# An attention block feeding a dense block on one core: when each load is issued, who fills the holes, and where block 1's decays stand

## The chip, the cores and the metric

The kernel runs on one core of a Trainium2 chip. The metric is the device time of one execution in microseconds; three runs of the kernel before gave 671.39 us in the median (670.71 to 673.25).

TensorE (PE) multiplies matrices into PSUM, VectorE (DVE) and ScalarE (ACT) work on tiles in SBUF and PSUM, GpSimd (POOL) is a fourth compute engine, and SyncE (SP) issues DMAs. ACT and POOL can issue DMAs too; each engine's instructions, DMA triggers included, are taken in the order in which they stand in its program.

## The reference

Two blocks in a row. The first is a linear attention with a decay per channel (RWKV-6), the second a dense layer with the activation `h - tanh(h)`:

```python
# r, k, v, w: (4, 8, 768, 48); u: (8, 48)
for t in range(S):
    cur = np.einsum('bhd,bhe->bhde', u[None] * kt, vt)
    y[:, :, t] = np.einsum('bhd,bhde->bhe', rt, state + cur)
    state = wt[:, :, :, None] * state + np.einsum('bhd,bhe->bhde', kt, vt)
...
x = attn_out.transpose(0, 2, 1, 3).reshape(4 * 768, 384)
h = x @ w_in            # 384 x 2048
out = (h - np.tanh(h)) @ w_out   # 2048 x 384
```

The attention's inputs and the output are float32; the dense weights come as float64.

## The kernel before

**Tiling.** The 3072 tokens are cut into 8 blocks of 384 (4 batches, 2 halves). The heads are worked on as 4 pairs, each pair on 128 partitions of which 96 carry data. Within a block, chunks of 64 tokens are solved by a tree: `level 1` and then levels m = 2, 4, 8, 16, 32 fill a matrix of scores from products of `kq` and `rp` (matmuls L242, and L319 for m = 32). After each level `decay` (L274) multiplies `kq` and `rp` in place by the running products of the decays, which `totals` (L260) makes from `wt`. Then `turn` transposes `kq` (L342, copied out at L344), `update` carries the state from chunk to chunk (L360, then DVE's chain of small operations L371), and `result` (L391, L409) makes the block's output, copied by ACT at L422 into `xT`, the input of the dense part. `late` holds the part of the output that does not fit the layout; six small DMAs of 24 KB (`fill_holes`, L429) put it into the holes of `xT`.

**Dense part.** For each block there are 16 steps f. A step has the product `hp` (L469) with one slice of `w_in`, six ACT operations (h, s, qa, qb, th, big, L476 to L481), five DVE operations that give `gT` (L486 to L494), and three steps later the products `acc` (L507) with one slice of `w_out`. `hp` has one PSUM buffer, so the next product waits until h has been read. At the end L512 copies `acc` out and a DMA stores it.

**Weights.** The float64 weights are read as pairs of 32-bit words, in 16 slices of 768 KB (`raw`, five buffers). `convert` turns a slice into float32 with two ACT operations (L170, L172) and two DVE operations (L174, L175).

**Order.** PE, SP, DVE and ACT run in the order in which the program emits; no scheduler moves anything on them. First `boot` does the whole attention of block 0 (in two halves of two pairs, `HALVES`), with the loads for block 1 and the first weights spread through it: `begin_behind(ins, dma)` makes a DMA wait for an instruction. In boot, six slices of weights are converted. Then, during the 16 dense steps of block i, the attention of block i + 1 runs a phase at a time: `plan(i)` says at which step each phase stands (`steps`), what DVE prepares before or behind a phase (`before`, `behind`), which steps convert a slice (`converted`), and which load is issued at which step (`loads`). In step f the order of emission is: `hp` and ACT's six operations of f, DVE's five operations of step f - 1 (with DVE's part of a conversion between them), what stands in `before`, the phase, what stands in `behind`, the load, ACT's part of a conversion, and `acc` of step f - 3.

All loads go through SP's queue, which is in order: a load that waits holds back everything behind it. Block 0's holes are filled by SP and ACT in turn, those of the other blocks by SP. Only block 0's step list (`i == 0`) has weights to load and convert.

Of the kernel before, what the change touches and what calls it, by code (L numbers as in the profile page):

```python
# [37 lines left out]
F32 = mybir.dt.float32  # L38
I32 = mybir.dt.int32
# [9 lines left out]
P = 128  # L49
# [35 lines left out]
def kernel(  # L85
# [23 lines left out]
    shift = const.tile([P, 3], F32, name="shift", tag="shift")  # L109
    for i, value in enumerate((QUAD[0][0], QUAD[1][0], -SMALL)):  # L110
        nc.vector.memset(shift[:, i:i + 1], value)

    warm = const.tile([P, 1], F32, name="warm", tag="warm")
    nc.scalar.activation(out=warm, in_=shift[:, 0:1], func=AF.Copy)
    u_sb = const.tile([P, NPAIR], F32, name="u_sb", tag="u_sb")
    nc.sync.dma_start(out=u_sb, in_=uT)


    masks = {}
# [63 lines left out]
    class Block:  # L183
# [16 lines left out]
        def load_v(self):  # L200
            self.v = inp.tile([P, NCP, DM], F32, name="v_sb", tag="v_sb")
            src = v[self.b, self.q * NB:(self.q + 1) * NB]
            nc.sync.dma_start(out=self.v, in_=src.rearrange("(c t) e -> t c e", t=P))

        def begin(self):
            self.xT = xpool.tile([P, KC, NB], F32, name="xT", tag="xT")
# [169 lines left out]
        def result(self, ps, pairs, holes_full=False):  # L376


            St, rp = states[self.q], self.tiles["rp"]
            yp = [scratch(ps) for e in range(2)]  # L380
            slots = [pairs[n:n + 2] for n in range(0, len(pairs), 2)]
            for n, slot in enumerate(slots):
                for c in range(NCP):
                    for par in range(2):
                        for p in slot:
                            for h in range(2):
                                rows = slice(64 * h, 64 * h + D)
# [12 lines left out]
            for n, slot in enumerate(slots):  # L400
                for p in slot:
                    for c in range(NCP):
                        for h in range(2):
                            for par in range(2):
                                toks = slice(64 * par, 64 * par + 64)
                                e0 = 64 * (h ^ (p % 2))
                                f0 = p * D2 + h * D
                                n0 = (n * NCP + c) * L
                                nc.tensor.matmul(yp[p % 2][e0:e0 + D, par, n0:n0 + L],  # L409
                                                 lhsT=self.v[toks, c, f0:f0 + D],  # L410
                                                 rhs=A[toks, h, p, c, :],
                                                 start=False,
                                                 stop=(n == len(slots) - 1 and c == NCP - 1),
                                                 skip_group_check=True)
            for n, slot in reversed(list(enumerate(slots))):
                for p in reversed(slot):
                    src = yp[p % 2][:, :, n * NCP * L:(n + 1) * NCP * L].rearrange(
                        "e a (c t) -> e c a t", t=L)
                    dst = self.xT[:, p, :] if p < KC else self.late
                    dst = dst.rearrange("e (c a t) -> e c a t", a=2, t=L)  # L420
                    for rows in (slice(0, D), slice(64, 64 + D)) if holes_full else (slice(0, P),):
                        nc.scalar.copy(out=dst[rows], in_=src[rows])  # L422

        def fill_holes(self, engines):

# [40 lines left out]
    def first(xT, f, ps):  # L466
        hp = ps.tile([P, NB], F32, name="hp", tag="hp")
        for kc in reversed(range(KC)):
            nc.tensor.matmul(hp, lhsT=w_in_sb[:, f, kc, :], rhs=xT[:, kc, :],  # L469
                             start=(kc == KC - 1), stop=(kc == 0))  # L470

        def new(name):
            return dense.tile([P, NB], F32, name=name, tag=name)

        h, th, s, qa, qb, big = (new(n) for n in ("h", "th", "s", "qa", "qb", "big"))
        nc.scalar.activation(out=h, in_=hp, func=AF.Copy, scale=1.0 / UPSCALE)  # L476
        nc.scalar.activation(out=s, in_=h, func=AF.Square)  # L477
        nc.scalar.activation(out=qa, in_=s, func=AF.Square, bias=shift[:, 0:1])  # L478
        nc.scalar.activation(out=qb, in_=s, func=AF.Square, bias=shift[:, 1:2])  # L479
        nc.scalar.activation(out=th, in_=h, func=AF.Tanh)  # L480
        nc.scalar.activation(out=big, in_=s, func=AF.Relu, bias=shift[:, 2:3])  # L481
        hs = dense.tile([P, NB], F32, name="hs", tag="hs", bufs=2)
        g = gpool.tile([P, NB], F32, name="gT", tag="gT")

        def product(out, in0, scalar, in1, op0):
            return lambda: nc.vector.scalar_tensor_tensor(out=out, in0=in0, scalar=scalar, in1=in1,  # L486
                                                          op0=op0, op1=ALU.mult)

        return g, [
            product(hs, h, SERIES, s, ALU.mult),  # L490
            lambda: nc.vector.tensor_tensor(out=th, in0=h, in1=th, op=ALU.subtract),  # L491
            product(hs, qa, QUAD[0][1], hs, ALU.add),
            product(g, qb, QUAD[1][1], hs, ALU.add),
            lambda: nc.vector.copy_predicated(out=g, mask=big.bitcast(I32), data=th)]  # L494

    class Second:

# [18 lines left out]
    def plan(i):  # L516

        names = ("level 1", 2, 4, 8, 16, 32, "turn", "update", "result")
        if i == 0:

            steps = (1, 2, 3, 4, 6, 8, 10, 11, 13)
            before = {0: ("totals 1", "totals 2", "kq")}
            behind, converted = {1: ("rp",)}, (0, 3, 3, 4, 4, 6, 10, 10, 12, 13)
            loads = {2: "weights", 5: "weights", 6: "weights", 7: "weights", 8: "weights",
                     9: "rmix", 10: "kmix", 11: "wt", 13: "kq", 14: "rp", 15: "v"}
        else:
            steps = (4, 5, 6, 7, 8, 9, 10, 11, 13)
            before = {0: ("kmix",), 1: ("rmix",), 2: ("totals 1",), 3: ("totals 2", "kq"), 4: ("rp",)}
            behind, converted = {}, ()
            loads = {5: "rmix", 7: "kmix", 9: "wt", 11: "kq", 14: "rp", 15: "v"}  # L530
        return dict(zip(steps, names)), before, behind, converted, loads

    blocks = [Block(b, q) for b in range(B) for q in range(NQ)]
# [16 lines left out]
    def boot(ps, blk, later):  # L550
# [21 lines left out]
        for m in (2, 4, 8, 16):  # L572
            blk.totals(m, h1, UP)
        masked()
        background = [lambda: later.load("rmix", rT, 0, NPAIR), lambda: later.load("kmix", kT, 0, NPAIR),
                      lambda: later.load("wt", wT, 0, NPAIR)] + [lambda: more_weights(nc.sync)] * 2
        ready, last = [], []
        for m in (2, 4, 8, 16, 32):
            for p0 in HALVES:
                if (m, p0) != (2, h1):  # L580
                    ins = blk.level(ps, m, p0, UP, last)
                if p0 == h2 or m == 32:
                    blk.totals(m, p0, UP)
            begin_behind(ins, background.pop(0)())
            if m <= 8:
                ready.append(convert(*raws.pop(0)))
            if m == 8:
# [2 lines left out]
        def converted():  # L590
            for op in ready.pop(0):
                op()

        for p0 in HALVES:
            blk.turn(ps, p0)
        for copies in last:
            copies()
        later.mix(0, NPAIR, ("kmix",))
        begin_behind(blk.update(ps, h1), later.load("kq", kT, 0, NPAIR))
        blk.update(ps, h2)  # L600
        blk.result(ps, [h1, h1 + 1])
        blk.fill_holes([nc.sync, nc.scalar])
        converted()
        ready.append(convert(*raws.pop(0)))
        more_weights(nc.sync)
        converted()
        blk.result(ps, [h2, h2 + 1], True)
        later.load("rp", rT, 0, NPAIR)
        more_weights(nc.sync)
        later.load_v()  # L610
        for _ in range(2):
            ready.append(convert(*raws.pop(0)))
        while ready:
            converted()
            more_weights(nc.sync)

    with tc.tile_pool(name="ps_boot", bufs=4, space=PSUM) as ps_boot:
        xT = blocks[0].begin()
# [4 lines left out]
    for i, blk in enumerate(blocks):  # L623
# [5 lines left out]
        phases, before, behind, converted, loads = plan(i)  # L629
        second = Second(blk.b * S + blk.q * NB, ps_d)  # L630
        for f in range(NF):
            g, next_rest = first(here, f, ps_d)
            waiting.append((second, f, g))

            for n, op in enumerate(rest):
# [6 lines left out]
            if later:  # L642
# [3 lines left out]
                    later.phase(ps_a, phases[f])  # L646
                for name in behind.get(f, ()):
                    later.prepare(name)
            name = loads.get(f)
            if name == "weights":  # L650
                more_weights(nc.sync)
            elif name and after:
                if name == "v":
                    after.load_v()
                else:
                    after.load(name, {"r": rT, "k": kT, "w": wT}[name[0]], 0, NPAIR)
            extra = []
            for _ in range(converted.count(f)):
                extra += convert(*raws.pop(0))
# [54 lines left out]
```

## Time and profile before

| | us |
|---|---|
| median of 3 runs | 671.39 (670.71 to 673.25) |
| the profiled execution, its own time | 671.54 |
| its span | 669.7 |
| first dense product of block 0 (PE L469) starts | 44.24 |
| first h (ACT L476) starts | 47.97 |
| block 1's level 1, level 2, level 4 on PE start | 50.64, 57.98, 64.58 |
| h of block 1's first step starts | 129.30 |
| h of the first step of blocks 2 to 7 starts | 207.55, 285.79, 365.03, 443.33, 521.58, 600.48 |

The times in the table are counted from the start of the span. From block 1 to block 6 a block takes some 78.3 to 79.2 us; block 0 takes 81.3 from its first h to block 1's first h, and 48 us of boot stand ahead of it.

| sums by engine, share of the span | us |
|---|---|
| PE | 642.5 (96%) |
| DVE | 545.4 (81%) |
| ACT | 488.8 (73%) |
| POOL, all of it in the first 4.2 us | 3.5 (1%) |

DMA moved 54.37 MB; SP's queue carried 52.82 MB of it. A load of 768 KB landed 4.5 (rmix, kq) to 7.9 us (wt) after its issue in the median, a slice of weights after 7.4.

In the views that follow, a line of the timeline gives the start in us, the time from the first to the end of the last of the merged instructions, the engine, the line of the kernel, the operation, what it writes and reads, the count, and in brackets the idle time before it and what ended it. "issue" means that the engine waited for nothing that the profile shows. A line of the windows gives a stretch, its length, the busy time of PE, its weight loads, DVE, ACT and POOL with counts, the granted clock of TensorE, the busy share of the DMA engines and GB/s.

### The profile page before, as it was taken

The numbers are of one execution on the slowest core, as the hardware profiler recorded it, in microseconds if no ns is written. First come the engines' busy times: TensorE is split into PE (matmuls) and PEld (weight loads), VectorE is DVE, ScalarE is ACT, GpSimd is POOL, SyncE is SP. The second block draws the span as 40 slices with busy tenths as digits, with TensorE's granted clock in tenths as the row PEclk, the third lists the DMA queues.
The fourth block names the chain that finished last, engine by engine and source line by source line (L and its number), as shares of the span: only waits on it lengthen the run. The fifth ranks groups of instructions, "written<-read, shape, count | busy, mean of one in ns | idle before, by whom it ended". The sixth has DMA issues, their size and how long they took to land.

```text
span 669.7 us, 19951 instructions
## 1 busy us (share of the span) xinstructions
PE 642.5 (96%) x8480; PEld 412.5 (62%) x8480; DVE 545.4 (81%) x1101; ACT 488.8 (73%) x966; POOL 3.5 (1%) x17
## 2 busy tenths in 40 slices
PE   5867999999999999999999999999999999999997
PEld 4745666566665666656665666656666566665554
DVE  7689998799778997599975998679976899756664
ACT  4676999775868667785776758677677857778785
POOL 2000000000000000000000000000000000000000
PEclk9977999999999999999999999999999999999999
DMA  8774620422102501214012131025011200000000
GB/s 317 241 267 204 234 98 2 139 97 84 48 9 87 178 2 49 87 42 144 2 49 92 62 119 45 9 89 178 4 49 32 97 2 3 2 10 36 1 0 36
DMA packets 30841, 54.37 MB, mean 81 GB/s; under 512 B 2336, under 2 KB 28704, under 8 KB 30752
## 3 DMA queue, kind: packets, MB, share of 16 engines
q1 hardware_dynamic: 30512, 52.82, 22.9%
q8 instruction: 67, 1.10, 0.7%
q10 hardware_dynamic: 240, 0.27, 0.1%
q14 instruction: 22, 0.18, 0.1%
HBM read 47.19 MB, written 4.72 MB: 78 GB/s over the span
## 4 chain that ended last, share of the span: by engine, by line
PE 81%; PEld 4%; issue 4%; DVE 4%; ACT 3%; DMA 2%; PEldq 1%; SPq 0%; ACTq 0%; DVEq 0%
PE acc L507 34%; PE hp L469 33%; PE att L242 9%; DVE states L371 2%; PE att L409 2%; PEld hp L469 2%; PE att L342 2%; PEld att L391 2%; PE att L319 1%; PEld acc L507 1%; DMA wt<-in_wT 1%; DMA xT<-late 1%; PEldq L397 0%; ACT qb L479 0%; ACT h L476 0%
## 5 line engine op out<-in xcount | busy, mean ns | idle before, releaser
L469 PE MATMUL hp<-xT,w_sb 128*128 128x384 f32 x768 | 272.4, 492 | 4.0 <-DMA xT<-late 2.5
L507 PE MATMUL acc<-w_sb,gT 128*128 128x384 f32 x768 | 273.8, 493 | 0.0
L469 PEld LDWEIGHTS hp<-xT,w_sb 128*128 128x128 f32 x768 | 147.0, 192 | 107.7 <-ACT h L476 3.4
L507 PEld LDWEIGHTS acc<-w_sb,gT 128*128 128x128 f32 x768 | 140.5, 190 | 88.7 <-ACT o L512 2.3
L476 ACT ACTIVATE h<-hp 128x384 f32<-128x384 f32 x128 | 62.7, 490 | 143.5 <-PE hp L469 142.8
L491 DVE TENSOR_TENSOR th<-h,th 128x384 f32<-128x384 f32 x128 | 71.0, 554 | 46.3 <-ACT th L480 46.3
L486 DVE SCALAR_TENSOR_TENSOR hs<-h,s 128x384 f32<-128x384 f32 x128 | 71.0, 555 | 26.0 <-ACT s L477 26.0
L494 DVE COPY_PREDICATED gT<-big,th 128x384 f32<-128x384 int32 x128 | 76.2, 595 | 12.5
L478 ACT ACTIVATE qa<-s,shift 128x384 f32<-128x384 f32 x128 | 78.8, 616 | 4.2
L486 DVE SCALAR_TENSOR_TENSOR gT<-qb,hs 128x384 f32<-128x384 f32 x128 | 71.4, 558 | 9.4
L481 ACT ACTIVATE big<-s,shift 128x384 f32<-128x384 f32 x128 | 76.8, 600 | 0.0
L479 ACT ACTIVATE qb<-s,shift 128x384 f32<-128x384 f32 x128 | 76.8, 600 | 0.0
L486 DVE SCALAR_TENSOR_TENSOR hs<-qa,hs 128x384 f32<-128x384 f32 x128 | 70.5, 551 | 0.0
L477 ACT ACTIVATE s<-h 128x384 f32<-128x384 f32 x128 | 67.0, 523 | 4.0
L242 PEld LDWEIGHTS att<-rp,kq 48*64 48x64 f32 x3072 | 54.7, 148 | 23.1 <-issue 16.9
L242 PE MATMUL att<-rp,kq 48*64 48x32 f32 x3072 | 58.8, 231 | 6.5 <-issue 4.4
L480 ACT ACTIVATE th<-h 128x384 f32<-128x384 f32 x128 | 64.9, 507 | 0.0
L274 DVE TENSOR_TENSOR kq<-kq,tot 128x768 f32<-128x768 f32 (+1 forms) x45 | 38.6, 859 | 4.2 <-PE att L242 2.3
L371 DVE SCALAR_TENSOR_TENSOR states<-states,tot,att 128x48 f32<-128x48 f32 x176 | 31.5, 257 | 9.1 <-PE att L360 9.1
L274 DVE TENSOR_TENSOR rp<-rp,tot 128x768 f32<-128x768 f32 (+1 forms) x45 | 38.8, 862 | 0.0
L302 DVE COPY_PREDICATED scores<-mask_all,att 128x384 f32<-128x384 uint8 (+1 forms) x54 | 31.9, 655 | 0.0
L242 PE MATMUL att<-rmix,kmix 48*64 48x64 f32 x768 | 14.5, 232 | 6.5 <-ACT rmix L222 6.5
(53 smaller groups left out, 335.4 us busy)
## 6 DMA issues: line engine op xcount, KB each, us to landing
raw<-in_weights SPq DMA_DIRECT2D x16, 768.0 KB, 7.4
rmix<-in_rT SPq DMA_DIRECT2D x7, 768.0 KB, 4.5
kmix<-in_kT SPq DMA_DIRECT2D x7, 768.0 KB, 7.1
wt<-in_wT SPq DMA_DIRECT2D x7, 768.0 KB, 7.9
kq<-in_kT SPq DMA_DIRECT2D x7, 768.0 KB, 4.5
rp<-in_rT SPq DMA_DIRECT2D x7, 768.0 KB, 4.7
v_sb<-in_v SPq DMA_DIRECT2D x8, 576.0 KB, 5.6
out_y<-o SPq DMA_DIRECT2D x23, 192.0 KB, 1.9
```

The costliest lines, as they stand in the source:

```text
L242: nc.tensor.matmul(dst, lhsT=lhs[rows, t0:t0 + L], rhs=src, start=True, stop=True)
L274: ins = nc.vector.tensor_tensor(out=part, in0=part, in1=by, op=ALU.mult)
L469: nc.tensor.matmul(hp, lhsT=w_in_sb[:, f, kc, :], rhs=xT[:, kc, :], start=(kc == KC - 1), stop=(kc == 0))
L477: nc.scalar.activation(out=s, in_=h, func=AF.Square)
L478: nc.scalar.activation(out=qa, in_=s, func=AF.Square, bias=shift[:, 0:1])
L479: nc.scalar.activation(out=qb, in_=s, func=AF.Square, bias=shift[:, 1:2])
L480: nc.scalar.activation(out=th, in_=h, func=AF.Tanh)
L481: nc.scalar.activation(out=big, in_=s, func=AF.Relu, bias=shift[:, 2:3])
L486: return lambda: nc.vector.scalar_tensor_tensor(out=out, in0=in0, scalar=scalar, in1=in1, op0=op0, op1=ALU.mult)
L491: lambda: nc.vector.tensor_tensor(out=th, in0=h, in1=th, op=ALU.subtract),
L494: lambda: nc.vector.copy_predicated(out=g, mask=big.bitcast(I32), data=th)]
L507: nc.tensor.matmul(acc, lhsT=g[:, j * P:(j + 1) * P], rhs=w_out_sb[:, f, :], start=(f == 0), stop=(f == NF - 1))
```

## The change

Six edits, all of them in the order and the triggers of loads and of preparations; nothing is computed otherwise.

- The load of `u_sb` moves from the head of SP's queue to ACT's, ahead of ACT's first operation.
- In boot, the loads behind the levels are named by level: rmix behind level 2 as before, kmix behind 8 (it was behind 4), wt behind 16 (it was 8), one slice of weights behind 32, and the next right after it without a trigger of its own (they were behind 16 and 32).
- kq of block 1 no longer starts behind the first half of block 0's `update`. The next slice of weights waits for the first of the copies of `result`'s second half (`copies[0]`), and kq, rp and another slice follow it in SP's queue. v of block 1 and four slices of weights leave boot.
- Block 0's holes are filled by SP, ACT and POOL, two each, instead of SP and ACT, three each.
- In the dense steps, every load waits for h of its own step (`made`). Nine slices of weights are loaded at steps 1 to 4 and 6 to 10 of block 0. v is loaded for the next block at step 5 (block 0) or 2, instead of for the block after it at step 15. The other loads of block 0's steps move by one or two steps.
- In block 0's steps, DVE's preparation at step 0 becomes totals 1, kq and rp; totals 2 moves behind level 1, where rp's decay stood. The conversions go from steps 0, 3, 3, 4, 4, 6, 10, 10, 12, 13 to 1, 3, 3, 4, 5, 7, 10, 10, 12, 13.

```diff
+    u_sb = const.tile([P, NPAIR], F32, name="u_sb", tag="u_sb")
+    nc.scalar.dma_start(out=u_sb, in_=uT)
 
     warm = const.tile([P, 1], F32, name="warm", tag="warm")
     nc.scalar.activation(out=warm, in_=shift[:, 0:1], func=AF.Copy)
-    u_sb = const.tile([P, NPAIR], F32, name="u_sb", tag="u_sb")
-    nc.sync.dma_start(out=u_sb, in_=uT)
...
         def load_v(self):
...
-            nc.sync.dma_start(out=self.v, in_=src.rearrange("(c t) e -> t c e", t=P))
+            return nc.sync.dma_start(out=self.v, in_=src.rearrange("(c t) e -> t c e", t=P))
...
+            copies = []
...
-                        nc.scalar.copy(out=dst[rows], in_=src[rows])
+                        copies.append(nc.scalar.copy(out=dst[rows], in_=src[rows]))
+            return copies[0]
...
-        nc.scalar.activation(out=h, in_=hp, func=AF.Copy, scale=1.0 / UPSCALE)
+        made = nc.scalar.activation(out=h, in_=hp, func=AF.Copy, scale=1.0 / UPSCALE)
...
-            before = {0: ("totals 1", "totals 2", "kq")}
-            behind, converted = {1: ("rp",)}, (0, 3, 3, 4, 4, 6, 10, 10, 12, 13)
-            loads = {2: "weights", 5: "weights", 6: "weights", 7: "weights", 8: "weights",
-                     9: "rmix", 10: "kmix", 11: "wt", 13: "kq", 14: "rp", 15: "v"}
+            before, behind = {0: ("totals 1", "kq", "rp")}, {1: ("totals 2",)}
+            converted = (1, 3, 3, 4, 5, 7, 10, 10, 12, 13)
+            loads = {f: "weights" for f in (1, 2, 3, 4, 6, 7, 8, 9, 10)}
+            loads.update({5: "v", 11: "rmix", 12: "kmix", 13: "wt", 14: "kq", 15: "rp"})
         else:
...
-            loads = {5: "rmix", 7: "kmix", 9: "wt", 11: "kq", 14: "rp", 15: "v"}
+            loads = {2: "v", 5: "rmix", 7: "kmix", 9: "wt", 11: "kq", 14: "rp"}
...
-        background = [lambda: later.load("rmix", rT, 0, NPAIR), lambda: later.load("kmix", kT, 0, NPAIR),
-                      lambda: later.load("wt", wT, 0, NPAIR)] + [lambda: more_weights(nc.sync)] * 2
+        background = {2: lambda: later.load("rmix", rT, 0, NPAIR), 8: lambda: later.load("kmix", kT, 0, NPAIR),
+                      16: lambda: later.load("wt", wT, 0, NPAIR), 32: lambda: more_weights(nc.sync)}
...
-            begin_behind(ins, background.pop(0)())
+            if m in background:
+                begin_behind(ins, background[m]())
...
+        more_weights(nc.sync)
         for p0 in HALVES:
             blk.turn(ps, p0)
         for copies in last:
             copies()
         later.mix(0, NPAIR, ("kmix",))
-        begin_behind(blk.update(ps, h1), later.load("kq", kT, 0, NPAIR))
-        blk.update(ps, h2)
+        for p0 in HALVES:
+            blk.update(ps, p0)
         blk.result(ps, [h1, h1 + 1])
-        blk.fill_holes([nc.sync, nc.scalar])
+        blk.fill_holes([nc.sync, nc.scalar, nc.gpsimd])
         converted()
         ready.append(convert(*raws.pop(0)))
-        more_weights(nc.sync)
         converted()
-        blk.result(ps, [h2, h2 + 1], True)
+        ins = blk.result(ps, [h2, h2 + 1], True)
+        begin_behind(ins, more_weights(nc.sync))
+        later.load("kq", kT, 0, NPAIR)
         later.load("rp", rT, 0, NPAIR)
         more_weights(nc.sync)
-        later.load_v()
         for _ in range(2):
             ready.append(convert(*raws.pop(0)))
         while ready:
             converted()
-            more_weights(nc.sync)
...
-            name = loads.get(f)
+            name, ins = loads.get(f), None
             if name == "weights":
-                more_weights(nc.sync)
+                ins = more_weights(nc.sync)
+            elif name == "v":
+                ins = later.load_v() if later else None
             elif name and after:
-                if name == "v":
-                    after.load_v()
-                else:
-                    after.load(name, {"r": rT, "k": kT, "w": wT}[name[0]], 0, NPAIR)
+                ins = after.load(name, {"r": rT, "k": kT, "w": wT}[name[0]], 0, NPAIR)
+            if ins:
+                begin_behind(made, ins)
```

From line 114 on the lines of the changed kernel differ by up to four from those of the kernel before: L469 becomes L471, L476 L478, L507 L509, L422 L423, L429 L431.

More of the change, by code (lines that the diff above doesn't have):

```diff
@@ L493, in first @@
             product(g, qb, QUAD[1][1], hs, ALU.add),
-            lambda: nc.vector.copy_predicated(out=g, mask=big.bitcast(I32), data=th)]
+            lambda: nc.vector.copy_predicated(out=g, mask=big.bitcast(I32), data=th)], made
     class Second:
@@ L631 @@
         for f in range(NF):
-            g, next_rest = first(here, f, ps_d)
+            g, next_rest, made = first(here, f, ps_d)
             waiting.append((second, f, g))
```

## The prediction

> **What bounds the kernel now.** I read the page first, then the waits, the chain and the timeline. The page says PE, 96%, and the waits say that ACT mostly waits for it:
>
> ```profile
> span 669.7 us, 19951 instructions
> PE 642.5 (96%) x8480; PEld 412.5 (62%) x8480; DVE 545.4 (81%) x1101; ACT 488.8 (73%) x966; POOL 3.5 (1%) x17
> PEclk9977999999999999999999999999999999999999
> ACT h L476 <- PE hp L469: 142.8, 104, 6.0
> ```
>
> The 96% is an average over two regimes. In the timeline of PE, matmuls follow one another from 64.58 on to the end. The holes that are left there are in the result matmuls L409, which take 2.55 us (block 0 and 3) and 2.24 (block 6) where the other blocks take 1.56. What matters is therefore when PE reaches 64.58, the level-4 matmuls of block 1 ("L4" below); 605.1 us follow whatever comes before. Loads in blocks 1 to 6 are hidden under that packed stream. So the sum is made of the first 64.58 us, where the timeline shows these lines:
>
> ```profile
> 25.80 0.43 PE L242 MATMUL att<-rp,kq 48*64 48x32 f32 x5 [1.59 <-issue]
> 26.28 0.56 DVE L274 TENSOR_TENSOR kq<-kq,tot 128x384 f32<-128x384 f32 x1 [2.09 <-PE att L242]
> ...
> 37.02 3.02 ACTq L429 DMA_DIRECT2D xT<-late  x3
> 38.94 1.09 SPq L162 DMA_DIRECT2D raw<-in_weights  x1
> 40.91 0.88 PE L409 MATMUL att<-scores,v_sb 64*48 64x64 f32 x21 [2.17 <-issue]
> 41.84 1.93 ACT L422 COPY xT<-att 48x384 f32<-48x384 f32 x4
> 44.24 3.63 PE L469 MATMUL hp<-xT,w_sb 128*128 128x384 f32 x6 [2.45 <-DMA xT<-late]
> 47.97 0.49 ACT L476 ACTIVATE h<-hp 128x384 f32<-128x384 f32 x1 [0.89 <-PE hp L469]
> 47.99 0.95 DVE L260 TENSOR_TENSOR tot<-wt 128x768 f32<-128x768 f32 x1
> ...
> 56.94 0.94 DVE L274 TENSOR_TENSOR rp<-rp,wt 128x768 f32<-128x768 f32 x1
> 57.98 2.79 PE L242 MATMUL att<-rp,kq 48*64 48x32 f32 x96 [2.63 <-issue]
> 60.70 3.94 PE L469 MATMUL hp<-xT,w_sb 128*128 128x384 f32 x6
> ```
>
> PE stands still twice with nothing to wait for (1.59 and 2.17 us, "issue"). Both times 768 KB (kmix, kq) were in flight, and a 16 KB packet of the instruction queue started only as they ended, at 23.39 and 38.62; PE went on about 1.3 us after it was read. ACT needs 3.02 us for three hole triggers, the last hole lands at 43.7, and PE starts the first product at half clock. Then DVE is the bound: from 47.99 it has almost no idle time, and level 2 at 57.98 waits for the decay of rp that ends at 57.88. Last the clock, in windows of 3.41 us:
>
> ```profile
> 36.95:40.35 3.40, 1.57 (x71) 1.30 (x72) 3.12 (x5) 0.69 (x3) 0.00 (x0) 1.00 0.68 235
> 40.35:43.77 3.42, 0.88 (x21) 0.66 (x20) 2.42 (x4) 3.34 (x6) 0.00 (x0) 0.50 0.78 264
> 54.00:57.42 3.42, 1.35 (x5) 0.47 (x3) 3.42 (x5) 3.35 (x8) 0.00 (x0) 1.00 1.02 428
> 57.42:60.83 3.41, 2.85 (x97) 2.81 (x97) 3.02 (x7) 1.30 (x3) 0.00 (x0) 0.50 0.25 100
> ```
>
> After the columns for PE to POOL come clock, DMA share and GB/s. A window with PE busy 1.57 or 1.35 us is followed by half clock, both times for 6.83 us (to 47.18 and 64.25).
>
> **The change, part by part.**
>
> u_sb on ACT's queue. SP's first load starts at 0.81 instead of 1.26; seven loads then go out every 0.51 us and DVE waits for wt. Gain 0.45. ACT pays one trigger of about 0.4 before its table load (0.81 to 2.09), and idles until kq at 4.5: nothing. If u came late, every L222 would wait; it landed 1.6 us after issue.
>
> kmix from level 4 to 8, wt from 8 to 16, weights 3 from 16 to 32. In the stage around 21.5 no load is then in flight, so the packet of 23.39 can start about 1.5 us earlier and the stall of 1.59 goes: gain 1.59 (bounds: 0, and DVE's 2.09). Against it, wt and weights 3 and 4 now run some 26 to 33.5, where the packet of 32.75 falls; a delay like the two above would give up to 1.5 back. I take 1.59 and keep the 1.5 for the range. So far 2.04.
>
> kq behind the update, and weights 5, rp, weights 6 and v, no longer run beside the holes. The stall of 2.17 shrinks, not to nothing: in block 0's result, with no load in flight, L409 still takes 2.55 for 1.56, a stall of 1.0. Gain 1.2. L409 ends at 41.79 - 2.04 - 1.2 = 38.55. ACT has two triggers instead of three: 34.98 + 0.61 + 0.85 = 36.5, a conversion of 1.7 (L170, L172) to 38.2, and the four copies 38.6 to 40.5. Two holes go to POOL, whose DMA this trace never shows. Bounds from the hole rows, issue to landing 1.8 to 5.5 us: two in series land between 38.6 and 46. I take the quiet 1.9 of SP's holes, as no load runs beside them; the first product may start at 40.6. At 46 it would cost up to 1.6 (a product at half clock, less the slack of h below).
>
> A rule speaks against POOL. DVE converts weights without a pause in that stage (L174 and L175, pairs of 1.4 us). The Trainium skill, SBUF — State Buffer, section "Who interferes with whom", has a VectorE instruction in a two-port mode shut GpSimd out for its whole length, and GpSimd writes the descriptors of POOL's DMAs. By the row above POOL costs nothing; by the rule the two holes land after a few conversions, still within the 46, so 0 to 1.6. No run here shows it.
>
> The new wait. SP now holds weights 5 until the first of the four copies, which ends at 39.1; queued behind it are kq, rp and weights 6. ACT waits for weights 5 in order, ahead of the first h; DVE's decays wait for kq and rp. Weights 3 and 4 landed 4.07 and 4.44 us after issue: 43.4. L170 and L172 take 1.71, to 45.1; DVE's last L175 follows by 0.98, so block 1's totals start at 46.0 (47.99 before), h at 45.15 (47.97). kq and rp, 768 KB each, take 2.0 us at the 401 GB/s that the windows show from 47.18 to 50.59, and land at 45.4 and 47.4; DVE wants them after the first two totals (1.43) at 47.4, and after kq's decay at 48.3. Cost nothing, covered by 2 and 1 us of DVE's work; with that gone, every us late is a us on DVE.
>
> Decays ahead of a conversion. From the totals at 47.99 to the end of level 2's decays at 62.65 DVE works 14.66 us, some 0.6 of it waits. The work stays the same: rp (0.88) and the small totals (1.1) change places, the conversion of weights 6 moves one step on. What goes is PE's delay: level 2 no longer waits for rp, and L4 hangs on DVE alone, where it hung on PE (62.65 against 64.58, with a product of 3.94 at half clock between). L4 at 46.0 + 14.4 = 60.4, a gain of 4.2.
>
> After L4. Before, PE reached level 16 3.3 us after its decays (79.90 against 76.57). DVE gains 2.0 and PE 4.2, so 1.1 is left; ACT loses one conversion (1.7) ahead of h7: no new stall. Weights 7 to 15 wait for h of their own step; one step (5.6 us with a level) plus the 3.0 of ACT's six ops covers the 4.4 landing. In blocks 1 to 6 every load has at least three steps, v nine; one step late would cost 5.6. The other edits only return handles.
>
> Sum: block 1's totals start 2.0 earlier (0.45, 1.59 and 1.2, of which the new wait for weights 5 takes 1.2 back), and 2.2 more comes from PE no longer trailing DVE; together 4.2. I take 4.0, for 0.2 of fresh waits in a tighter stage: 671.54 (this execution: span 669.7 and 1.84 around it) - 4.0 = 667.5. The median of the runs is 671.39, 0.15 lower, and they spread over 2.5, so I do not correct for it.
>
> **The rivals.**
>
> Half clock reaches into the packed part (0.22). At full clock PE is early: from h at 45.15 come a product (2.2), level 1 (1.65) and a product (2.2), then level 2 needs a buffer that DVE frees at 52.5 (46.0 + totals 1.43 + decays 1.76 + five ops 2.4 + half of L249's copies 0.95), then level 2 (1.6) and a product (2.2): 56.3. It idles 4.1 us to L4, more than the 2.6 that set off the second throttle. If so, about 5 of the 6.83 us lie after 60.4 and cost 2.6: 670.0. Against it: between 38.6 and 45.6 PE has 2 us of work, which throttles it until 49 to 53, stretches its work by up to 3.4, and so fills the idle time. The Trainium skill, TensorE: Matmul & The Clock Gate, "What's actually happening", says that the window runs free of the kernel, so its phase would differ from run to run; this one profile cannot show that.
>
> It doesn't do what it says (0.15). The instruction packets queue behind wt and weights 3 and 4 instead, 1.5 comes back, DVE's slack is used up, and with part of the clock loss: about 670.5. For it: the loads are the same bytes, only 6 us later.
>
> Slower (0.11). Weights 5 is the new wait of ACT. The landing times of raw are 4.1, 7.4 in the median, 12.0 at most. L4 is back at 64.58 when the totals start at 50.2, so when weights 5 lands at 47.6, 8.5 us after its issue; at 12.0 it is 3.5 late: 675.0, and up to 2.6 more with the clock. Against it: it is first in an empty queue, while 7.4 belongs to rows of several loads.
>
> **How the numbers follow.** The forecast, 667.5, has 0.52, and by itself reaches from 665.0 (the L409 stalls of 1.0, 1.0 and 0.7 realigned, on top) to 668.0. The rivals at 670 and 670.5 stretch the range to 671.4; the slow one is left out. This kernel's measurement tells 0.5%, 3.4 us, from no change: faster 0.52, within 0.37, slower 0.11.
>
> **What would show it.** Right: no issue wait over 1 us near 24, the four copies of 48 partitions done by about 40.5, h first at 45 to 46, L4 at 60 to 61 and matmuls without holes after it. Wrong: an ACT wait for raw of more than 3 us before the first h, a wait of PE's first product for xT after 43, DVE waiting for kq or rp, or half clock after L4.

## The result and the profile after

The changed kernel takes 672.57 us in the median of four runs (672.34 to 673.40), the kernel before 672.17 on the same chip (670.71 to 673.25, four runs). The ratio is 1.001 with a 95% interval of 0.9986 to 1.0033: no difference that can be measured. The forecast was 667.5, and its range ended 1.2 us short.

The profiled execution took 672.34 us with a span of 670.6, against 671.54 and 669.7 before. The head of its page:

```profile
span 670.6 us, 19961 instructions
PE 643.4 (96%) x8480; PEld 413.0 (62%) x8480; DVE 545.1 (81%) x1101; ACT 489.0 (73%) x966; POOL 5.0 (1%) x19
PEclk9968999999999999999999999999999999999999
```

PE is busy 0.9 us longer for the same 8480 matmuls, and the clock row has lost tenths in other slices than before. The rest of the reading is in the timeline. First the boot, up to block 1's first totals:

```profile
24.63 0.43 PE L242 MATMUL att<-rp,kq 48*64 48x32 f32 x5 [0.44 <-issue]
25.10 0.56 DVE L274 TENSOR_TENSOR kq<-kq,tot 128x384 f32<-128x384 f32 x1 [0.93 <-PE att L242]
...
35.37 0.33 PE L391 MATMUL att<-rp,states 48*64 48x64 f32 x3 [1.39 <-issue]
36.75 0.48 ACT L423 COPY late<-att 128x384 f32<-128x384 f32 x1 [2.10 <-PE att L409]
37.25 1.23 SPq L431 DMA_DIRECT2D xT<-late  x2
37.26 1.50 ACTq L431 DMA_DIRECT2D xT<-late  x2
37.28 1.54 PE L391 MATMUL att<-rp,states 48*64 48x64 f32 x44 [0.49 <-ACT late L423]
37.52 1.49 POOL L431 DMA_DIRECT2D xT<-late  x2 [33.34 <-ACT late L423]
38.94 1.53 PE L409 MATMUL att<-scores,v_sb 64*48 64x64 f32 x48
40.55 1.94 ACT L423 COPY xT<-att 48x384 f32<-48x384 f32 x4
41.05 0.33 SPq L162 DMA_DIRECT2D raw<-in_weights  x1
42.54 4.21 PE L471 MATMUL hp<-xT,w_sb 128*128 128x384 f32 x6 [2.07 <-ACT xT L423]
45.42 0.90 ACT L170 ACTIVATE w_sb<-raw 128x768 f32<-128x768 f32 x1 [1.22 <-DMA raw<-in_weights]
47.14 0.49 ACT L478 ACTIVATE h<-hp 128x384 f32<-128x384 f32 x1
48.02 0.95 DVE L260 TENSOR_TENSOR tot<-wt 128x768 f32<-128x768 f32 x1
```

Both issue stalls of before are gone: 1.59 us became 0.44 (DVE's decay behind it runs at 25.10, not 26.28), and the matmuls of L409 at 38.94 no longer stop for 2.17. But a new stall of 1.39 stands at 35.37, between them. With it `late` is copied at 36.75, 0.23 later than before, and the copies at 40.55 release the slice of weights at 41.05. That slice lands 4.35 us later, ACT waits for it, and the totals start at 48.02, where they started at 47.99. The first product starts 1.7 us earlier than before and waits for the copies, no longer for a hole. One more thing delays the copies: the half clock now begins at 37.31 instead of 40.35, and the 44 matmuls of L391 behind `late` take 1.54 us for the 0.92 of before:

```profile
37.05 0.92 PE L391 MATMUL att<-rp,states 48*64 48x64 f32 x44 [0.49 <-ACT late L422]
```

From there to block 1's level 4 ("L4", at 64.58 before), and the clock windows around it:

```profile
55.11 1.60 PE L242 MATMUL att<-rp,kq 48*64 48x32 f32 x96
...
62.36 2.79 PE L242 MATMUL att<-rp,kq 48*64 48x32 f32 x96 [3.47 <-DVE rp L274]
65.08 3.65 PE L509 MATMUL acc<-w_sb,gT 128*128 128x384 f32 x6
```

```profile
54.37:57.78 3.41, 3.41 (x103) 2.38 (x102) 3.31 (x9) 3.35 (x7) 0.00 (x0) 1.00 0.50 158
57.78:61.20 3.42, 1.11 (x4) 0.36 (x2) 3.42 (x6) 3.35 (x8) 0.00 (x0) 1.00 0.71 237
61.20:64.61 3.41, 2.25 (x85) 2.28 (x88) 3.41 (x6) 3.41 (x7) 0.00 (x0) 0.50 0.54 210
64.61:68.03 3.42, 3.42 (x26) 2.14 (x22) 3.28 (x6) 0.86 (x2) 0.00 (x0) 0.50 0.00 0
68.03:71.44 3.41, 3.41 (x67) 2.07 (x67) 3.41 (x8) 0.71 (x2) 0.00 (x0) 1.00 0.00 0
```

Level 2 stands at 55.11 instead of 57.98: it no longer waits for rp. Then PE has nothing to do until DVE's decays of level 2 end, 3.47 us, and L4 follows at 62.36, 2.2 us earlier than before. But the window from 57.78 has PE busy for 1.11 us only, the next two are at half clock (the column ahead of the last two: 0.50), and they lie on L4 and the products behind it: 2.79 us for 1.60, and 3.65 for 2.20. Before, the half clock ended at 64.25, just ahead of L4.

So the time went as follows (starts in us from each span's start):

| | before | after | ahead of before |
|---|---|---|---|
| first totals of block 1 | 47.99 | 48.02 | 0.0 |
| level 4 of block 1 | 64.58 | 62.36 | 2.2 |
| first h of block 1 | 129.30 | 129.27 | 0.0 |
| first h of block 7 | 600.48 | 601.52 | -1.0 |
| end of the span | 669.7 | 670.6 | -0.9 |

The last microsecond is lost in blocks 3 and 6: the result matmuls L409 take 2.61, 3.10 and 2.96 us in blocks 0, 3 and 6, where they took 2.55, 2.55 and 2.24, and 1.56 in the blocks without a stall. In block 3 the line is, after and before:

```profile
353.08 0.54 PE L409 MATMUL att<-scores,v_sb 64*48 64x64 f32 x21 [1.23 <-issue]
352.64 0.54 PE L409 MATMUL att<-scores,v_sb 64*48 64x64 f32 x21 [0.68 <-issue]
```

### The profile page after: what moved, and what is told of

Same layout as the page of the kernel before. It is cut to its first block, busy times and chain, and to the rows that moved or that the text cites. A ratio compares the mean times of both kernels' runs of the same rounds, so it can differ in the third digit from the quotient of the medians.

```text
span 670.6 us, 19961 instructions
## 1 busy us (share of the span) xinstructions
PE 643.4 (96%) x8480; PEld 413.0 (62%) x8480; DVE 545.1 (81%) x1101; ACT 489.0 (73%) x966; POOL 5.0 (1%) x19
## 4 chain that ended last, share of the span: by engine, by line
PE 76%; DVE 8%; issue 4%; PEld 4%; ACT 4%; DMA 2%; PEldq 1%; SPq 0%; DVEq 0%; ACTq 0%
PE acc L509 33%; PE hp L471 30%; PE att L242 8%; DVE states L371 2%; PE att L409 2%; PEld att L391 2%; PEld hp L471 2%; PE att L342 2%; PEld acc L509 1%; PE att L319 1%; DMA kq<-in_kT 1%; DVE rp L274 1%; DVE w_sb L175 1%; DVE hs L488 1%; DMA raw<-in_weights 1%
## 5 line engine op out<-in xcount | busy, mean ns | idle before, releaser
L471 PE MATMUL hp<-xT,w_sb 128*128 128x384 f32 x768 | 272.6, 492 | 3.0 <-ACT xT L423 2.1
L509 PE MATMUL acc<-w_sb,gT 128*128 128x384 f32 x768 | 275.2, 495 | 0.0
L471 PEld LDWEIGHTS hp<-xT,w_sb 128*128 128x128 f32 x768 | 147.2, 192 | 106.6 <-issue 2.4
L509 PEld LDWEIGHTS acc<-w_sb,gT 128*128 128x128 f32 x768 | 141.2, 191 | 89.5 <-ACT o L514 2.3
L478 ACT ACTIVATE h<-hp 128x384 f32<-128x384 f32 x128 | 62.9, 491 | 143.2 <-PE hp L471 142.5
L488 DVE SCALAR_TENSOR_TENSOR hs<-h,s 128x384 f32<-128x384 f32 x128 | 71.0, 554 | 27.2 <-ACT s L479 27.2
L488 DVE SCALAR_TENSOR_TENSOR gT<-qb,hs 128x384 f32<-128x384 f32 x128 | 71.4, 558 | 9.2
L488 DVE SCALAR_TENSOR_TENSOR hs<-qa,hs 128x384 f32<-128x384 f32 x128 | 70.5, 551 | 0.0
L274 DVE TENSOR_TENSOR kq<-kq,tot 128x768 f32<-128x768 f32 (+1 forms) x45 | 38.6, 857 | 2.8 <-PE att L319 1.6
```

The lines of the kernel that those rows point to most:

```text
L274: ins = nc.vector.tensor_tensor(out=part, in0=part, in1=by, op=ALU.mult)
L509: nc.tensor.matmul(acc, lhsT=g[:, j * P:(j + 1) * P], rhs=w_out_sb[:, f, :], start=(f == 0), stop=(f == NF - 1))
```

## The experiments

Two questions were open: what made the new stall at 35.37, which ate the gain of the boot, and whether the half clock ate the 2.2 us at L4. Each kernel below is the changed kernel with one edit, except the last, which has several. Executions of one kernel already differ in boot: the very first decay of DVE starts between 6.33 and 7.07 us in the eight profiles that have `u_sb` on ACT's queue. So later stages are compared by distances between two points of one profile: from the copy of `late` to block 1's first totals (11.27 us in the changed kernel, 11.47 before), and from those totals to block 1's first h (81.25, and 81.31 before). These distances differ between executions too: the first lies between 10.86 and 11.46 in five profiles whose kernels do not differ there, the second between 80.32 and 81.52 in five profiles whose dense steps are those of the changed kernel. The ratios below are to the kernel before, which was run again beside them; the changed kernel itself was not.

### Four products to keep PE busy ahead of L4

```diff
+                if i == 0 and f == 3:
+                    second.acc = [ps_d.tile([P, DM], F32, name=f"acc{j}", tag=f"acc{j}", bufs=1)
+                                  for j in range(NB // P)]
+                    for _ in range(4):
+                        nc.tensor.matmul(second.acc[0], lhsT=w_in_sb[:, 0, 0, :], rhs=here[:, 0, :],
+                                         start=True, stop=True)
```

(Not shown: the first `add` of this block then takes over these accumulators and does not make new ones.) The result of these products is overwritten by the first product of `acc`; they are work added, nothing else.

> Adds four products of 128x384 (into the accumulators that the dense part clears afterwards; the output is the same) on PE ahead of block 1's level 4, where the changed kernel's PE idles from 58.9 to 62.4. Theory: that idle time brings the half clock of 61.2 to 68.0, and the half clock is what gave the gain back. Then level 4 still starts near 62.4 but takes 1.6 instead of 2.8 us, the products behind it 2.2 instead of 3.65, and the span falls by about 2.6 us, to about 668. Rival: DVE is the bound and the clock hardly matters: the stream behind level 4 then waits for DVE's decays and the span stays within 0.7 us of 670.6. Rival: the half clock comes from the boot's low activity and not from this gap: then it comes all the same, the four products take 1.3 us each and push level 4 to about 64, and the span is about 672.

Measured: 669.61 us in the median of 10 runs, ratio 0.997 to before (0.9955 to 0.9985). The windows of this kernel:

```profile
54.79:58.20 3.41, 2.04 (x99) 1.85 (x99) 3.31 (x8) 3.35 (x7) 0.00 (x0) 1.00 0.37 124
58.20:61.61 3.41, 3.41 (x7) 1.90 (x6) 3.41 (x7) 0.96 (x3) 0.00 (x0) 0.50 0.43 178
61.61:65.03 3.42, 3.42 (x71) 2.06 (x71) 3.42 (x5) 3.36 (x7) 0.00 (x0) 1.00 0.56 190
```

and PE's timeline there:

```profile
61.28 2.91 PE L652 MATMUL acc<-xT,w_sb 128*128 128x384 f32 x8
64.12 1.60 PE L242 MATMUL att<-rp,kq 48*64 48x32 f32 x96
65.65 2.20 PE L509 MATMUL acc<-w_sb,gT 128*128 128x384 f32 x6
```

(L652 is the added line.) The half clock still comes, but it is one window long and over before L4, which again takes 1.60 and the products 2.20. From the totals to block 1's first h this kernel takes 78.96 us, the changed one 81.25: 2.3 us won by adding work. In the five profiles with the changed kernel's steps L4 takes 1.84 to 2.79 us, so the full clock here is hardly a lucky position of the windows alone; and the ten runs agree. So the half clock on L4 and behind it is the cost of the gap ahead of L4. Filling the gap brings 1.4 to 2.6 us against those five profiles; the prediction's rival had 2.6. The price of the added products is small but not nothing: L4 comes 14.9 us behind the totals instead of 14.3.

### Less DVE work ahead of L4

```diff
-            before, behind = {0: ("totals 1", "kq", "rp")}, {1: ("totals 2",)}
-            converted = (1, 3, 3, 4, 5, 7, 10, 10, 12, 13)
+            before, behind = {0: ("totals 1", "kq", "rp")}, {3: ("totals 2",)}
+            converted = (2, 3, 3, 4, 5, 7, 10, 10, 12, 13)
```

> Moves two things that DVE does ahead of block 1's level-4 matmuls behind them: the small totals (1.1 us) and the conversion of the seventh slice of weights (1.4 us). Theory: DVE alone sets level 4's start. It then starts 2.5 us earlier, near 59.9, PE idles about 1 us instead of 3.4, no half clock follows, and the span falls by 4 to 5 us, to about 666. Rival: the half clock comes anyway: level 4 at 59.9 but the span falls only by 2 to 2.5. Rival: something else holds level 4 (a PSUM buffer, a load): no change of its start.

Measured: 669.20 us, median of 10 runs, ratio 0.9963 (0.9944 to 0.9982). In PE's timeline the wait ahead of L4 is half as long:

```profile
61.55 2.19 PE L242 MATMUL att<-rp,kq 48*64 48x32 f32 x96 [1.65 <-DVE rp L274]
63.67 3.21 PE L509 MATMUL acc<-w_sb,gT 128*128 128x384 f32 x6
```

L4 comes 12.3 us behind the totals (14.3 in the changed kernel), so DVE does set it. A half clock still follows, now one window (62.32 to 65.73) and not two: L4 takes 2.19 and the products 3.21. Totals to block 1's first h: 78.39 us, 2.9 less than the changed kernel and 1.9 to 3.1 less than the five profiles. The theory had no half clock and a span of about 666; the profile has 668.1. In this execution the stall of the boot, 1.39 in the changed kernel, was 2.47 (33.70 to 36.17); the gain was made in spite of it.

### The fifth slice of weights behind the holes

```diff
-        more_weights(nc.sync)
         for p0 in HALVES:
             blk.turn(ps, p0)
...
         blk.fill_holes([nc.sync, nc.scalar, nc.gpsimd])
+        more_weights(nc.sync)
```

> Moves one of the two 768 KB slices of weights that run from 30 to 35 us in the boot to behind the hole transfers. Theory: PE's 1.39 us without a reason at 34 is its instruction packet queued behind these slices. With one of them gone the packet starts by about 32.5 instead of 33.14 and the idle time falls below 0.8 us, so the first copy of the result starts at 36.1 or earlier instead of 36.75. Rival: the packet is late for a reason of its own: 1.4 us stay. The span says little here, as the moved slice then delays the next one.

Measured: 671.29 us in one run. The timeline where the stall stood, first PE, then ACT:

```profile
33.56 0.33 PE L391 MATMUL att<-rp,states 48*64 48x64 f32 x3 [0.30 <-issue]
33.97 1.53 PE L409 MATMUL att<-scores,v_sb 64*48 64x64 f32 x48
```

```profile
35.59 0.48 ACT L423 COPY late<-att 128x384 f32<-128x384 f32 x1 [1.65 <-PE att L409]
...
42.11 0.90 ACT L170 ACTIVATE w_sb<-raw 128x768 f32<-128x768 f32 x1 [0.79 <-DMA raw<-in_weights]
45.42 0.89 ACT L170 ACTIVATE w_sb<-raw 128x768 f32<-128x768 f32 x1 [1.60 <-DMA raw<-in_weights]
47.12 0.49 ACT L478 ACTIVATE h<-hp 128x384 f32<-128x384 f32 x1
```

The stall is gone. The DMA records say why: PE's instruction queue reads 16 KB at a time, and in all nine profiles with the changed boot's order PE goes on 1.3 to 1.5 us after a packet has been read. That packet starts 5.5 us behind the one before it here (31.37 after 25.85), 6.7 in the changed kernel (33.14 after 26.48), and 6.7 to 7.9 in the six other kernels that load the fifth slice where the changed one does. In those seven the fourth and fifth slices (the prediction's weights 3 and 4), 768 KB each, are in flight then, issued at 28.2 and 28.6 and landed at 33.26 and 35.68 in the changed kernel, and PE stalls for 1.4 to 2.5 us in every one. The last kernel of this section, which moves the fifth slice too, has 5.7 between the packets and no such stall either.

But the time did not improve by it: `late` is at 35.59 (0.7 of the 1.16 us is an earlier first decay, 6.35) and the totals again at 48.00, 12.4 us behind it and not 11.3. The slice that was moved now lands late, and the one behind it too, and ACT waits for both (0.79 and 1.60). The stall has become a wait for weights, so this edit alone is worth nothing at the totals.

### u_sb back on SP's queue

```diff
-    nc.scalar.dma_start(out=u_sb, in_=uT)
+    nc.sync.dma_start(out=u_sb, in_=uT)
```

> Puts the load of u back at the head of SP's queue, all else as in the changed kernel. Theory (the one of the prediction): all that hangs on the first loads is 0.45 us later, DVE's first decay at 7.6 instead of 7.14. Rival, from the traces of both kernels: the first loads are held by the slowest of the DMA engines and not by SP's triggers, so the first decay stays at 7.1 to 7.2 and nothing later moves.

Measured: 673.07 us in one run; DVE's first decay starts at 7.78, in the changed kernel at 7.07. Over all profiles it is 7.09 and 7.78 with u on SP (the first is the kernel before), and 6.33 to 7.07, in the mean 6.67, with u on ACT. That points the way of the forecast, but the two values with u on SP lie 0.7 apart themselves: neither the 0.45 nor the rival, no effect, is shown.

### DVE's order as before

```diff
-            before, behind = {0: ("totals 1", "kq", "rp")}, {1: ("totals 2",)}
-            converted = (1, 3, 3, 4, 5, 7, 10, 10, 12, 13)
+            before, behind = {0: ("totals 1", "totals 2", "kq")}, {1: ("rp",)}
+            converted = (0, 3, 3, 4, 4, 6, 10, 10, 12, 13)
```

> Undoes one part of the change: DVE prepares block 1 in the old order (both totals and kq at step 0, rp behind level 1) and the conversions stand at their old steps. Theory: this part alone let level 2 start 2.9 us earlier (55.1 against 58.0) and shortened the idle time ahead of it; undone, level 2 waits again for rp's decay, near 58, and level 4 starts near 64, counted with block 1's totals at 48; block 1's first h comes out within 1 us of the changed kernel's, since with the old order the half clock falls on the boot of block 1 and not on the stream. Rival: the part was worth what it moved: block 1's first h 2 to 3 us later.

Measured: 671.11 us in one run. Totals to block 1's first h: 80.51 us, against 81.25 with the new order. Level 2 is late again (10.0 us behind the totals, 7.1 in the changed kernel) and L4 1.0 later behind them, yet nothing is lost, because the half clock then falls ahead of L4 (at 63.67, with its 1.60 us):

```profile
56.53:59.95 3.42, 1.63 (x97) 1.62 (x97) 3.39 (x6) 2.83 (x6) 0.00 (x0) 1.00 0.81 293
59.95:63.36 3.41, 3.41 (x6) 1.67 (x6) 3.31 (x6) 0.00 (x0) 0.00 (x0) 0.50 0.08 32
63.36:66.77 3.41, 3.41 (x102) 2.53 (x102) 3.27 (x7) 2.92 (x6) 0.00 (x0) 1.00 0.43 133
```

80.51 lies within what executions differ by. So no worth of the decays ahead of the conversion, alone, can be seen: what they bring on DVE, the gap that they open on PE takes back.

### The holes on two queues

```diff
-        blk.fill_holes([nc.sync, nc.scalar, nc.gpsimd])
+        blk.fill_holes([nc.sync, nc.scalar])
```

> Undoes one part of the change: block 0's holes go through SP and ACT, three each, POOL has none. Theory: POOL's holes were not late (both landed by 40.3, two us ahead of the first product), and ACT pays one trigger more, 0.6 to 1.4 us, ahead of the conversion and of the four copies; the copies, the trigger of the sixth slice behind them, and block 1's totals come that much later. Rival: the third queue was worth nothing, as PE is later than ACT: copies and totals at the same distance from the late copy (4.5 and 11.3 us).

Measured: 671.40 us in one run. ACT's timeline:

```profile
37.30 2.22 ACTq L431 DMA_DIRECT2D xT<-late  x3
39.56 0.91 ACT L170 ACTIVATE w_sb<-raw 128x768 f32<-128x768 f32 x1 [1.91 <-issue]
```

A third trigger costs ACT 0.72 us (2.22 against 1.50), and the four copies come 4.37 us behind `late`; in all eight other kernels of the changed order it is 3.80 or 3.81. So the third queue is worth 0.6 us at the copies. The totals come 11.80 behind `late`, 0.3 to 0.9 later than in the five profiles that do not differ there.

### The sixth slice of weights without a wait

```diff
-        begin_behind(ins, more_weights(nc.sync))
-        later.load("kq", kT, 0, NPAIR)
+        w5 = more_weights(nc.sync)
+        begin_behind(ins, later.load("kq", kT, 0, NPAIR))
```

> The sixth slice of weights no longer waits for the copies; it goes out behind SP's two holes, some 2.5 us earlier, and kq takes over the wait. Theory: this slice is the new wait that holds block 1's totals: they come 1.1 to 2 us earlier, counted from the late copy (9.3 to 10.2 us behind it instead of 11.3). Rival: the slice collides with the holes on the DMA engines, the first product starts later, and the totals come no earlier.

Measured: 670.27 us in one run. ACT's two pairs of conversions follow each other without a wait:

```profile
43.95 0.89 ACT L172 ACTIVATE up<-raw 128x768 int32<-128x768 uint32 x1
44.74 0.89 ACT L170 ACTIVATE w_sb<-raw 128x768 f32<-128x768 f32 x1
```

and the totals start 9.97 us behind `late`, 1.3 less than in the changed kernel. The added wait costs 0.9 to 1.5 us at the totals, by the five profiles that have it; the prediction had 1.2.

### All that helped, together

Small totals behind level 4, the fifth slice behind the holes, the sixth converted in step 2, and kq and rp in the queue ahead of the sixth and seventh slice:

```diff
-            before, behind = {0: ("totals 1", "kq", "rp")}, {1: ("totals 2",)}
-            converted = (1, 3, 3, 4, 5, 7, 10, 10, 12, 13)
+            before, behind = {0: ("totals 1", "kq", "rp")}, {3: ("totals 2",)}
+            converted = (2, 3, 4, 4, 5, 7, 8, 10, 10, 12, 13)
...
-        more_weights(nc.sync)
         for p0 in HALVES:
...
         blk.fill_holes([nc.sync, nc.scalar, nc.gpsimd])
+        more_weights(nc.sync)
...
-        begin_behind(ins, more_weights(nc.sync))
-        later.load("kq", kT, 0, NPAIR)
+        begin_behind(ins, later.load("kq", kT, 0, NPAIR))
         later.load("rp", rT, 0, NPAIR)
-        more_weights(nc.sync)
         for _ in range(2):
-            ready.append(convert(*raws.pop(0)))
+            more_weights(nc.sync)
+        ready.append(convert(*raws.pop(0)))
```

> Takes together what the runs point to: the small totals behind level 4; the fifth slice of weights loaded behind the holes (no packet delay at 34); the sixth converted during step 2 and no longer ahead of the first h, and the others one to two steps later; kq and rp ahead of the sixth and seventh slice. Theory: block 1's totals start 3 us earlier, near 45, level 4 hangs on PE alone and starts at 57 to 59, no half clock falls behind it, and the span is 663 to 666, 0.9 to 1.3% below the changed kernel. Rival: DVE's moved work (2.5 us and one more conversion of 1.4) is wanted back by level 8 and 16, the stream waits there, and the span is no lower than 668.

Measured: 669.65 us in the median of 12 runs (667.14 to 673.16), before 672.59 beside it (17 runs), ratio 0.9957 (0.993 to 0.9984). The profiled execution took 667.98 with a span of 665.9:

```profile
45.23 0.95 DVE L260 TENSOR_TENSOR tot<-wt 128x768 f32<-128x768 f32 x1
...
48.29 0.96 DVE L274 TENSOR_TENSOR rp<-rp,wt 128x768 f32<-128x768 f32 x1 [0.64 <-DMA rp<-in_rT]
```

```profile
58.27 1.64 PE L242 MATMUL att<-rp,kq 48*64 48x32 f32 x96
59.84 2.20 PE L509 MATMUL acc<-w_sb,gT 128*128 128x384 f32 x6
61.88 2.10 PE L471 MATMUL hp<-xT,w_sb 128*128 128x384 f32 x6
65.43 1.60 PE L242 MATMUL att<-rp,kq 48*64 48x32 f32 x96 [1.46 <-DVE rp L274]
```

The totals are 2.8 us ahead of before, L4 6.3, PE comes to it without a gap and at full clock, and block 1's first h stands at 125.82, 3.5 ahead. Some 0.8 of each is that DVE's first decay was earlier in this execution (6.33, before 7.09). By distances the gain lies between `late` and the totals, 9.38 us for 11.47 before; from the totals to block 1's first h it is 80.59, within what executions of the changed kernel's steps show. Both failed steps of the prediction are gone from it. What is missing between the 6.3 at L4 and the 3.5 at the first h went into later gaps, which the lead over the other engines opened: level 8 waits 1.46 us for DVE's decays, and a product at 92.60 waits 1.17 for ACT's h. Some 0.4% under the kernel before is shown. The theory's span of 663 to 666 is reached by this execution and two others of the twelve; their median is near 667.6. Nor is the median below those of the two kernels that mend the gap ahead of L4 alone (669.61 and 669.20), so what the other edits add in time is not shown.

## Why the prediction was wrong

By its own steps, in the profiled execution unless said otherwise:

| step | predicted | measured |
|---|---|---|
| u_sb on ACT's queue | 0.45 earlier | 0.0 here; 0.8 between the means of all profiles, not shown |
| first issue stall (1.59) goes | 1.59 | 1.2 |
| packet of 32.75 behind weights 3 and 4 | 0, bound 1.5 | a stall of 1.39; 1.4 to 2.5 in all that have it |
| second issue stall (2.17) shrinks | by 1.2 | it went altogether |
| two holes on POOL | 0, bound 1.6 | 0: all holes landed by 40.31, nobody waited |
| landing of the slice behind the copies | 4.07 to 4.44 after issue | 4.35, issued 2 us later than forecast |
| kq and rp hidden behind totals and decays | 0 | 0 (landed 47.5 and 49.6; wanted 49.5 and 50.4) |
| totals to L4 | 14.4 | 14.34 |
| half clock behind L4 | none (rival: 2.6) | 1.19 on L4 and 1.45 on the products, 2.6 |
| later loads, blocks 1 to 6 | 0 | no wait for a load; 1.0 in the stalls of L409, with no load in flight |

Two steps failed; by the sum, either alone would have left a gain of 1.5 to 2 us.

The first is in the paragraph on the loads behind the levels: "a delay like the two above would give up to 1.5 back. I take 1.59 and keep the 1.5 for the range". The bound was right for this execution and the value chosen, nothing, was wrong: the prediction moved the loads out of the way of one instruction packet and into the way of the next. (It had these loads end at 33.5; the fifth slice landed at 35.68.) The kernel with the fifth slice behind the holes shows it: there the stall is 0.30. The copies came at 40.55, where 38.6 was forecast, and the slice that waits for the first copy passes every microsecond on to the totals: 48.02, where 46.0 was forecast. These 2 us are the new stall (1.4), the rest of the first stall (0.4), the 0.45 of `u_sb` that did not show in this execution and 0.6 for L391 at half clock, which the sum did not have, less the 1.0 that the second stall gave above what was counted.

The second is the argument against its own rival "Half clock reaches into the packed part": that an earlier throttle would stretch PE's work and so fill the idle time. It did throttle PE earlier, from 37.31 to 50.96, but level 1, level 2 and two products ran at full clock after that, and PE stood idle for 3.47 us. From there on the rival's chain came true link by link, with its 2.6 us. The prediction gave the rival's time as 670.0, on top of totals at 46.0; with totals 2 us later the same sum gives 672.0, and the profiled execution took 672.34. That this comes so near is in part luck: the 1.0 us of blocks 3 and 6 is in the 672.34 and not in the sum.

Right were the mechanisms: that most of the first stall was a packet behind a load (0.44 of 1.59 stays with the load gone), that the order on DVE frees level 2 (57.98 to 55.11) and leaves L4 to DVE, the price of the new wait (1.2 forecast, 0.9 to 1.5 by the kernel without it), and that the loads tied to their own step cost nothing in blocks 0 to 6. The rule that the prediction weighed (the Trainium skill, SBUF — State Buffer, "Who interferes with whom": a two-port instruction of VectorE shuts GpSimd out) cost nothing that could be seen here: while DVE ran L174 and L175 without a pause, POOL's two triggers took 1.49 us, as ACT's 1.50, and its holes landed 2.0 us after issue in the median, SP's 1.9, ACT's 2.3. The profile does not name the mode in which an instruction ran; L174 takes 0.55 us for 768 columns, as long as L488 takes for 384, so it may have been such a one.

The stalls of L409 in blocks 3 and 6 are packets of instructions too. In all ten profiles a packet of 16 KB starts 1.2 to 1.9 us ahead of each of these stalls, and PE goes on 1.2 to 1.5 us after it has been read; in the 4 us ahead of the stalls in blocks 3 and 6 no load moved a byte. So a packet can stop PE without a load beside it, here for 0.3 to 1.2 us. The matmuls of L409 take 2.17 to 3.10 us there, with no order by kernel, so the lost microsecond of blocks 1 to 6 may be a matter of the execution and not of the change. Open stays why these packets start so late.

## What to carry to other kernels

Work that is brought forward on one engine can open a gap on another, and on TensorE the gap had a price of its own here, 2.6 us, that fell on what came next; before a gap is opened ahead of a packed part, look how busy PE will be in the window before, and fill it or close it. A load that is moved out of the way of one instruction packet can land on the next, as it did here: list the times of all packets, not that of the stalled one alone. And a stage that waits for a load whose trigger waits for the stage itself passes every delay on, so a saving in front of it is only worth what the trigger sees of it.

## What the runs showed of the hardware

**How little idle time halves the clock.** The ten profiles were cut into the 3.41 us windows that the clock's changes mark, and PE's busy time was summed in each window at full clock between 9 us and 79. Of 17 windows with PE busy up to 1.85 us, 16 were followed by half clock; none with 2.25 or more was; between 2.0 and 2.2 both happened. So in this kernel it needs no idle window, only one in which PE is little more than half busy (1.85 of 3.41 us): 1.65 us of waiting was enough in the kernel with less DVE work, and a wait of 3.47 gave two windows of half clock. The windows have no fixed place: in four kernels that are the same up to 48 us, the first half clock began 3.7 us ahead of the copy of `late` to 0.6 behind it. That agrees with the free-running window that the Trainium skill tells of (TensorE: Matmul & The Clock Gate, "What's actually happening").

**A load in flight can stop matmuls that need none of it.** With two slices of 768 KB in flight, a packet of 16 KB of instructions started 1.0 to 2.4 us later than in the two kernels without the second of them, and PE stood still for 1.4 to 2.5 us with nothing else to wait for; without it the stall was 0.3. The packets themselves cost 0.3 to 1.2 us in blocks 3 and 6 with no load in flight.

**Adding four products of 128x384 made the kernel faster**: 0.3% under the kernel before (0.9955 to 0.9985), where the changed kernel without them is at 1.001 (0.9986 to 1.0033) on another chip.
